# A fused DeltaNet and MLP-Mixer kernel: another order of its job pieces from the 705th on

## The chip, the cores and the metric

The kernel runs on one core of one Trainium2 chip. The metric is the device time of one execution in microseconds (us), as the median of several runs. PE is TensorE (PEld its weight loads), DVE VectorE, ACT ScalarE, POOL GpSimd, and SP the engine whose queue issues the DMAs.

## The reference, cut to what matters

Four batches of 768 positions go through a DeltaNet recurrence with 8 heads of 48 features. Its output, seen as 768 x 384 for each batch, goes through an MLP mixer with a token part and a channel part. Everything is fp32.

```python
k_n = k / (np.linalg.norm(k, axis=-1, keepdims=True) + 1e-06)
for t in range(S):                      # S = 768, state is 48 x 48 per head
    y[:, :, t] = q_t @ state
    state = state + beta_t * outer(k_t, v_t - state.T @ k_t)
...
h = np.maximum(x.T @ w_tok1, 0.0) @ w_tok2      # x: (768, 384) of one batch
u = x + h.T
out = u + np.maximum(u @ w_ch1, 0.0) @ w_ch2    # 384 -> 1536 -> 384
```

## The kernel before, in words

The recurrence is worked in chunks of 64 positions, two chunks to a unit u of 128, so there are 24 units and 48 chunk steps t, twelve to a batch. The kernel is written as jobs, each a Python generator that issues a few instructions and yields; one such stretch is a *piece*. There are 2543 pieces. One long string, `order` (line 1239), says by hand in which order the pieces are issued: `r12*5` means five pieces of job r12. Nothing is reordered after that. Each engine, and SP's DMA queue, works through its own instructions in the order of the string, and waits with semaphores where it needs another's result. So the string alone decides what stands ahead of what on each engine.

The jobs that matter here:

- `k{u}`, `v{u}` load keys, queries and values by SP's queue. The last piece of `v{u}` scales the values on POOL (line 426).
- `p{u}` prepares norms and scales; `c{u}` (and `d{u}` for the first twelve units) forms the Gram matrices on PE as small tiles (line 453, tile p_g), four pieces, and scales them on DVE (line 459).
- `t{u}` sends the triangular blocks to DRAM, `i{n}` inverts them for a round of up to four units on DVE (lines 681 and 686: a pair of dependent operations to a piece, 30 pairs), and `f{u}` fetches them back (line 653). `j{u}` joins the half blocks on PE in 32-row tiles (lines 785 to 834).
- `r{t}` is one chunk step of the recurrence, below.
- `m{b}` is the mixer of batch b: full 128-row tiles on PE, in lines 1060, 1073, 1083 (turns), 1140 for the first batch, 1032 for the others (a fast product with 15 sums in place of 18 products), and 1162. DVE adds the results (1044, 1077, 1091), ACT copies and clips.
- `w{j}` rounds one piece of the weights; `s` sums weight blocks; `x`, `z`, `Y` keep PE warm.

A step of the recurrence is a chain across engines, with a piece at almost every link:

```python
for p, i, r, _ in heads:                               # "k": 8 matmuls, four pieces
    nc.tensor.matmul(p_k[r, p], kqt[f, p, cc, 0], s0[f, p])                    # L862
nc.vector.tensor_tensor(out=rest, in0=p_k, in1=vsts[u][:, :, cc], ...)         # L869
for p, i, r, o in heads:                               # "y": 16 matmuls
    nc.tensor.matmul(p_y[o, p], kqt[f, p, cc, 1], s0[f, p], ...)               # L882
    nc.tensor.matmul(p_w[r, p], gm[r, 2 * p + cc, TC], rest[r, p])             # L886
nc.scalar.copy(w_t, p_w)                                                       # L892
for p, i, r, o in heads:                               # "s": 16 matmuls
    nc.tensor.matmul(p_s[PAR[i], p], gm[r, 2 * p + cc, 0:C], w_t[r, p])        # L900
    nc.tensor.matmul(p_y[o, p], gm[r, 2 * p + cc, GC], w_t[r, p], ...)         # L901
nc.vector.tensor_tensor(out=s1, in0=s0, in1=p_s, op=ALU.subtract)              # L909
nc.scalar.mul(y[...], p_y[...], ...)                                           # L914
```

The step t + 1 begins with the state s1 of step t. Each matmul of fp32 shows as two records in the profile, so k has 16 records and y and s have 32 each, of 48 or 64 rows and 64 columns. A whole step is ten pieces: four for k, then rest, y, w_t, s, s1 and the output. The first step of a batch (t = 0, 12, 24, 36) has no k and starts from the values. The text calls the bursts of step 31 k31, y31 and s31. Mixer b can start once the steps of its batch are written, and its pieces are put between the bursts of the later steps.

PE's work is thus of two kinds: full 128 x 128 tiles (mixer, transposes) and small tiles (Gram, joins, recurrence).

Of the kernel before, what the change touches and what calls it, by code (L numbers as in the profile page):

```python
# [23 lines left out]
def kernel(  # L24
# [1217 lines left out]
    c1*2 d1 k2 p2*2 c1 t0 d1 c1*2 d1*3 t0 p2*8 c2*2 w2 d2 c2*3 Y d2 w2 k3*6 p3 d2*2  # L1242
    p3 d2 t1*3 x p3*7 c3 k4*5 k7 w13 w18*2 d3*2 v1*2 v0*2 c3*3 v0 c3 d3*3 t0 p4*2
    t2*3 x t3*2 p4*2 x t3 i0*2 w13 p4*2 w18 w17*2 i0 k4 i0*9 p4 i0*2 p4*2 c4 k8
    c4*3 w13*2 w6*2 k5*2 v0 k6 k5*2 i0*2 d4*2 k5 x z d4*3 c4 z*2 p5*2 k5 t4 p5 h0
    h1 h0 w8*2 h1 Y i0 f0 Y p4 f1 h2*2 p5*3 f0*2 w6 h0*5 k6*5 p6 z f2*2 k8*3 p5 w6
    p5 p3 p5 j0*3 f1*2 h1*5 j0*2 w8*2 w17 f2 h2*3 v0 t4*2 w17 r0*5 p6 h2*2 c5*2 v1
    w11*2 j1 p5 k7*2 c5 k7 c5 r0 c5 r0*2 w14*2 v1 w11*2 k7*2 p7 d5*5 r1*5 w14*2
# [28 lines left out]
    r21*3 p15 r21*2 p16*4 j12 j13 k17*3 r21 j12 r21 p16 k17*3 m0*3 r21*3 m0 r22*2
    k17 r22 v11 k17 r22 k17*3 c16*4 r22*3 m0 c16*2 r22*3 t15 m0 r23*4 s p17*2 r23
    p16 p17*3 m0 p17 r23 k17 p17 t16 p17 m0*2 t16*2 t14*3 c17*2 t16 c17*3 r23 t14
    r23 c17 m0*2 s m0*3 t15*3 t17 s*4 t17*3 s*2 k18 m0*3 f12 i4*2 r23 i4*3 m0*2 i4  # L1280
    m0*2 v12*4 i4*2 k18 v12 k18*2 i4 k18 j13 m0*2 j13 r24*5 f13 j13*2 i4*4 r24 m0
    k18 m0*2 k18*2 v13*2 k18*2 r24 i4*2 k18*2 p18*2 i4 m0*3 r25 p18*2 r25*3 p18 i4
# [14 lines left out]
    m1*3 p23 m1*2 r35 m1 r35 p23*2 m1*6 t22*2 m1*2 c23*3 m1*2 c23*2 r35 c23 m1 v18
    f18*2 m1 t23*4 m1*2 r35 m1*6 j18*3 v18 j19 m1 v18 j19 f20 m1 j20 i6*4 f19 m1*3
    v18 j19 r36*4 j20 i6*2 r36*4 i6*5 m2 r37*3 f20 r37*2 i6*2 v20 f21 m2*2 f21 j21
    f21 r37*2 m2 i6*2 r37 m2*2 r37 r38*4 j20 i6*5 v19*5 r38 m2*2 r37 i6*4 r38 j21  # L1300
    r38*3 m2*3 r39*5 r38 m2*3 r39*2 m2*7 r39*2 m2*4 r40 j21 r40*4 i6 v21 i6*6 m2*2
    i6 r39 v21 m2*7 r40*2 j21*2 r40*3 m2 r41*5 m2*5 r41*2 m2*5 r41*3 m2*3 f22 m2
# [42 lines left out]
```

## Time and profile before

| | before |
|---|---|
| time, median of 3 runs | 639.9 us (639.62 to 640.89) |
| span of the profiled execution, first to last instruction | 636.9 us |
| PE busy | 608.5 us, 96% |
| DVE busy | 447.9 us, 70% |
| ACT busy | 268.0 us, 42% |
| POOL busy | 107.2 us, 17% |
| mean granted TensorE clock | 0.976 |

The times of the profile count from the span's start. The span is 3.0 us shorter than the median of the runs: the runs' time also holds what lies around the first and last instruction. A busy PE is an engine with some matmul in its pipeline; the time that it loses between matmuls of different kinds counts as busy too, so such losses have to be read from the starts of the matmuls and not from the busy share.

### The profile page before, as it was taken

The numbers are of one execution on the slowest core, as the hardware profiler recorded it, in microseconds if no ns is written. First come the engines' busy times: TensorE is split into PE (matmuls) and PEld (weight loads), VectorE is DVE, ScalarE is ACT, GpSimd is POOL, SyncE is SP. The second block draws the span as 40 slices with busy tenths as digits, with TensorE's granted clock in tenths as the row PEclk, the third lists the DMA queues.
The fourth block names the chain that finished last, engine by engine and source line by source line (L and its number), as shares of the span: only waits on it lengthen the run. The fifth ranks groups of instructions, "written<-read, shape, count | busy, mean of one in ns | idle before, by whom it ended". The sixth has DMA issues, their size and how long they took to land.

```text
span 636.9 us, 21542 instructions
## 1 busy us (share of the span) xinstructions
PE 608.5 (96%) x9132; PEld 531.5 (83%) x9132; DVE 447.9 (70%) x1132; ACT 268.0 (42%) x693; POOL 107.2 (17%) x146
## 2 busy tenths in 40 slices
PE   8488988899999999999999999999999999999997
PEld 5367877668898988859889999769999987999997
DVE  4987876967999658988969987776728253373643
ACT  7758785447523342215624323325334130232240
POOL 2348354235210211111111001000010000000000
PEclk9978796999999999999999999999999999999999
DMA  9686666666543355344454223202020000000000
GB/s 201 127 148 151 153 142 153 162 135 162 110 113 89 71 116 101 76 109 79 90 103 95 43 82 58 48 5 42 5 53 2 27 2 0 26 1 26 2 26 26
DMA packets 135776, 50.27 MB, mean 79 GB/s; under 512 B 114656, under 2 KB 130144, under 8 KB 135680
## 3 DMA queue, kind: packets, MB, share of 16 engines
q1 hardware_dynamic: 135680, 48.89, 35.2%
q8 instruction: 72, 1.18, 0.8%
q14 instruction: 24, 0.20, 0.1%
HBM read 39.42 MB, written 9.44 MB: 77 GB/s over the span
## 4 chain that ended last, share of the span: by engine, by line
PE 82%; DVE 7%; ACT 4%; DMA 3%; issue 2%; POOL 1%; SPq 1%; ACTq 0%; DVEq 0%; POOLq 0%
PE p_o L1162 26%; PE p_r L1032 20%; PE p_c L1140 8%; PE p_h L1073 5%; PE p L1060 4%; PE p_k L862 3%; PE p_g L453 3%; PE p_y L882 3%; PE p_s L900 3%; PE p_w L886 1%; DVE sub L681 1%; DVE x L686 1%; PE p_y L901 1%; PE p_ut L1083 1%; PE p_z L785 1%
## 5 line engine op out<-in xcount | busy, mean ns | idle before, releaser
L1162 PE MATMUL p_o<-wc,r 128*128 128x192 f32 x720 | 126.1, 329 | 0.6 <-ACT u_t L1087 0.6
L1162 PEld LDWEIGHTS p_o<-wc,r 128*128 128x128 f32 x720 | 116.8, 190 | 2.7 <-ACT u_t L1087 1.1
L1044 DVE TENSOR_TENSOR r<-r,p_r 128x512 f32<-128x512 f32 x90 | 59.8, 684 | 38.1 <-PE p_r L1032 34.3
L1091 DVE TENSOR_TENSOR xb<-xb,p_o 128x192 f32<-128x192 f32 x84 | 29.3, 350 | 57.8 <-PE p_o L1162 57.3
L1041 ACT COPY r<-p_r 128x512 f32<-128x512 f32 x54 | 31.3, 585 | 85.7 <-PE p_r L1032 76.1
L686 DVE TENSOR_TENSOR x<-x,sub 128x84 f32<-128x84 f32 (+24 forms) x178 | 59.4, 334 | 6.1
L681 DVE TENSOR_TENSOR sub<-x 128x84 f32<-128x84 f32 (+24 forms) x178 | 58.0, 326 | 6.8 <-DMA x<-n_dram 2.3
L1162 PE MATMUL p_o<-wc,s 128*128 128x192 f32 x288 | 51.5, 331 | 0.3 <-DVE xb L1091 0.3
L1140 PE MATMUL p_c<-u_t,wc 128*128 128x256 f32 x216 | 51.0, 386 | 0.2 <-ACT u_t L1087 0.2
L1162 PEld LDWEIGHTS p_o<-wc,s 128*128 128x128 f32 x288 | 46.7, 190 | 1.4 <-DVE xb L1091 0.6
L1048 ACT ACTIVATE r<-r 128x512 f32<-128x512 f32 x54 | 34.0, 631 | 26.7 <-DVE r L1044 26.2
L426 POOL TENSOR_TENSOR v_st<-v_st,nrm 128x384 f32<-128x384 f32 x24 | 20.1, 838 | 146.3 <-DMA v_st<-in_v_dram 109.3
L1140 PEld LDWEIGHTS p_c<-u_t,wc 128*128 128x128 f32 x216 | 39.7, 190 | 6.0 <-ACT u_t L1087 0.4
L516 POOL TENSOR_TENSOR mb<-mask_c,cs 128x512 f32<-128x512 f32 x20 | 21.2, 1062 | 138.9 <-DVE cs L494 138.6
L914 ACT ACTIVATE xb<-p_y 64x192 f32<-64x192 f32 x96 | 31.2, 325 | 23.6 <-PE p_y L901 12.2
L892 ACT COPY w_t<-p_w 128x192 f32<-128x192 f32 x48 | 15.2, 316 | 58.0 <-PE p_w L886 57.5
L1032 PE MATMUL p_r<-u_t,wc 128*128 128x128 f32 x288 | 38.7, 277 | 0.0
L453 PE MATMUL p_g<-kq 48*64 48x128 f32 (+1 forms) x704 | 33.6, 281 | 3.8 <-ACT kq L529 3.3
L1032 PE MATMUL p_r<-t_d,wc 128*128 128x128 f32 x288 | 37.3, 280 | 0.0
L1032 PEld LDWEIGHTS p_r<-u_t,wc 128*128 128x128 f32 x288 | 35.3, 192 | 0.4
L1060 PE MATMUL p<-xb,w 128*128 128x384 f32 x96 | 34.9, 511 | 0.0
L1032 PEld LDWEIGHTS p_r<-t_d,wc 128*128 128x128 f32 x288 | 34.0, 192 | 0.8
(184 smaller groups left out, 1212.2 us busy)
## 6 DMA issues: line engine op xcount, KB each, us to landing
d<-in_moe_w_ch_dram SPq DMA_DIRECT2D x24, 384.0 KB, 3.5
v_st<-in_v_dram SPq DMA_DIRECT2D x96, 48.0 KB, 2.7
out_dram<-xb SPq DMA_DIRECT2D x23, 192.0 KB, 1.9
kst<-in_k_dram SPq DMA_DIRECT2D x64, 48.0 KB, 2.9
n_dram<-gm SPq DMA_DIRECT2D x72, 32.0 KB, 2.4
pads<-in_k_dram SPq DMA_DIRECT2D x24, 96.0 KB, 2.9
pads<-in_q_dram SPq DMA_DIRECT2D x24, 96.0 KB, 2.9
gm<-w_dram SPq DMA_DIRECT2D x72, 32.0 KB, 2.1
```

Source lines behind the costliest of these rows:

```text
L453: nc.tensor.matmul(p_g[PAR[i ^ cc], p], kqt[f, p, cc, 0], kqt[f, p, cc])
L681: nc.vector.tensor_tensor(out=tmp, in0=y[:, :, 0:s, s : s + 1].to_broadcast([n, k, s, w]), in1=y[:, :, s : s + 1, s + 1 : m].to_broadcast( ...
L686: nc.vector.tensor_tensor(out=y[:, :, 0:s, s + 1 : m], in0=y[:, :, 0:s, s + 1 : m], in1=tmp, op=ALU.add,)
L914: nc.scalar.mul(y[:, :, D * i : D * i + D], p_y[PAR[1 - i]], 1.0 if c else -1.0)
L1032: nc.tensor.matmul(p[:, i], pieces[i // width][:, at : at + 128], f[f"u{n}"], start=first and i == 0, stop=True, skip_group_check=True,)
L1041: nc.scalar.copy(o, p)
L1044: nc.vector.tensor_tensor(out=o, in0=o, in1=p, op=ALU.add if sign > 0 else ALU.subtract)
L1048: nc.scalar.activation(o, o, ACTF.Relu)
L1060: nc.tensor.matmul(p_1[dh], piece_of(w1, c, 0)[:, dh * 128 : (dh + 1) * 128], xb[:, c], start=(c == 0), stop=(c == NCH - 1),)
L1073: nc.tensor.matmul(p_h, piece_of(w2, j, c * 128)[:, c * 128 : (c + 1) * 128], r1[j], start=(j == 0), stop=(j == NDH - 1),)
L1140: nc.tensor.matmul(p_c[:, k], piece_of(wc1, cb, f * 128)[:, f * 128 : (f + 1) * 128], u_t[:, cb], start=(cb == 0), stop=(cb == NCB - 1),)
L1162: nc.tensor.matmul(p, a[:, m], wc2[:, m, j], start=(start and i == 0), stop=(i == NM - 1), skip_group_check=True,)
```

## The change

Only the string `order` changes. The first 704 pieces and the last 159 (all of mixer 3) stand as before; between them the same pieces come in another order. Each job's own pieces keep their order, and every engine gets the same instructions as before, with the same shapes. In the new string more pieces with small tiles, of the Gram, join and recurrence jobs, stand next to each other, where the old one has a mixer piece between them. The first part and the end of the change, as they stand in the two strings (lines of the diff that only break differently are left out):

```diff
-    ... k11*2 v5 r10*3 i2 w4 i2*3 w15*3 w19*2 i2 w19 m0
-    i2 w12 r10*2 m0*2 r11 r10 p11 k12*4 w19 p11 p10 k12*2 p12 Y i2 w25 r11*3 d10*4
-    r11*2 v7 c10*3 w15 k12 i2*2 w21 i2*4 v6*3 r11*2 i2*3 k11 r11 v7*4 i2*4 c10
+    ... k11*2 v5 w15 p10 m0 k12 w12 w15 i2*3 r10*3
+    i2*4 k12 w4 k11 m0 r10 w12 w25*2 w12 i2 m0 r10 r11 k12*3 r11 c10 r11*2 r10
+    i2*2 w12 r11 i2*10 c10*3 w21 f7 k12 f6 d10 c10 r11*2 d10 p11 f6*2 d10*2 r11*2
...
-    r12 m0 w23*4 j8 r12 t10 r12 t10*2 r13 p10 w23 r13*4 w20*2 p11*3 p12*2 w20*2
+    j6*2 m0 j7*3 w25 v6 w25*4 v6 f9 m0 v6 w20 p10 w27 r12*5 p12 r12*3 p11 c11 w27
+    c11*4 w20*2 w21*2 r13*4 m0 r13*3 w20 f8*2 j8 t10*3 j8*2 k12 w15 f8 f9 k12
...
-    r30*3 t18*4 f17*2 f16 t19*2 c20*3 t20*3 r31*5 p21*3 m1*2 r31 p21
-    r31*3 c21*2 p21 c21 m1 t19 j17 t20 c21*3 m1 t21*4 r32*4 m1*12 j17 m1 v16*4 r32
+    p20*2 m1*4 r30 m1 c20 r30*2 r31*2 k21*6 p21*2 r31*3 c20*5 t20*2 r31 t20*2 m1
+    v16*2 m1 v16*3 m1 r31*3 p21*4 r31 m1*14 k22*2 r32*5 m1*3 k22 m1*2 p21 r32*2
+    m1*3 r32*2 k22 c21*2 r33*4 r32 r33 c21*4 t18 r33*2 m1 t18 k22*4 p21 k22*4
+    p22*3 r33*3 j17*2 p22*2 r34*4 v17*5 r34 m1*2 p22*2 r34*2 c22*2 r34*3 c22*3 Y
...
-    m2*2 f23*3 j23 r43*2 m2*6 f23 m2*11 v22 m2*4 r43*2 j23 r44*2 r43 r44 j23 r44
-    m2*5 v22*4 r44*3 m2*3 r44*3 m2*5 r45*5 m2*9 r45*2 j23 r45*3 m2*2 j23 m2*9 p23
-    v23*3 m2 r46*4 m2*2 v23*2 r46 m2*9 r46*2 m2*2 r46*3 m2*7 r47*5 m2*6 r47 m2 r47
-    m2*2 r47 m2*6 r47 m3*6 m2*5 m3*6 m2*11 m3*3 m2 m3*159
+    r42 r41 r42*4 m2 r42 m2 r42*3 m3 r42 r43*4 f22*3 j22*2 r43*3 m3 f23*3 r43 f22
+    j23 j22 j23*2 r43*2 r44 f23 r44*3 v22*5 m3 r44*6 j23*2 r45*9 r46*2 r45 v23*5
+    r46*8 m2 r47*5 m3 r47*4 m3*170
```

The mixer pieces that stood between the bursts of steps 44 to 47 now stand earlier or later in the string.

More of the change, by code (lines that the diff above doesn't have):

```diff
@@ L1241 @@
     w10 p0*2 z w3 w2 c0*3 p0 w3*2 d0*2 w3 c0 p1 c0 d0*3 k2*3 v1 p1*2 w18 k2*2 p1*2
[L1242 to L1248, printed above, removed]
+    c1*2 d1 k2 p2*2 c1 t0 d1 c1*2 d1*3 t0 p2*8 c2*2 w2 d2 c2*3 Y d2 w2 k3*6 p3
+    d2*2 p3 d2 t1*3 x p3*7 c3 k4*5 k7 w13 w18*2 d3*2 v1*2 v0*2 c3*3 v0 c3 d3*3 t0
+    p4*2 t2*3 x t3*2 p4*2 x t3 i0*2 w13 p4*2 w18 w17*2 i0 k4 i0*9 p4 i0*2 p4*2 c4
+    k8 c4*3 w13*2 w6*2 k5*2 v0 k6 k5*2 i0*2 d4*2 k5 x z d4*3 c4 z*2 p5*2 k5 t4 p5
+    h0 h1 h0 w8*2 h1 Y i0 f0 Y p4 f1 h2*2 p5*3 f0*2 w6 h0*5 k6*5 p6 z f2*2 k8*3 p5
+    w6 p5 p3 p5 j0*3 f1*2 h1*5 j0*2 w8*2 w17 f2 h2*3 v0 t4*2 w17 r0*5 p6 h2*2 c5*2
+    v1 w11*2 j1 p5 k7*2 c5 k7 c5 r0 c5 r0*2 w14*2 v1 w11*2 k7*2 p7 d5*5 r1*5 w14*2
     p6*2 t5 j1 t5*2 r1*2 j1 j2 p7 h3*2 r1*3 p6*3 i1*2 r2*5 k8*2 f3*2 w9 k9*3 j1*2
@@ L1257 @@
     w29 w27*2 r8*2 w29*3 j4*2 r8 w22*4 t9*4 r8*3 p10 h5*2 k11 h5 j5 Y i2 r9*3 r8
-    r9*2 i2*4 j5 i2*3 r9*2 i2 h5 k12*2 j5 Y r9*2 m0 v6 k11 j5 p9 w4*2 r10*3 i2*2 j5
-    k10 r10 p10*4 w4 v5 i2 v5*3 r9 k11*2 v5 r10*3 i2 w4 i2*3 w15*3 w19*2 i2 w19 m0
-    i2 w12 r10*2 m0*2 r11 r10 p11 k12*4 w19 p11 p10 k12*2 p12 Y i2 w25 r11*3 d10*4
-    r11*2 v7 c10*3 w15 k12 i2*2 w21 i2*4 v6*3 r11*2 i2*3 k11 r11 v7*4 i2*4 c10
-    k12*3 m0*4 c10 m0*2 w25 m0 w12 d10 f6*4 f7*2 p11*2 m0*3 w12 w21 w12 p12 p11*2
-    m0*2 f7 w21*2 j6*2 j7 v6 p12 w25*3 f8*2 w27*2 m0 j6 j7*2 m0 r12*5 f8 f7 j8*2
@@ L1277 @@
[L1277 to L1282, printed above, removed]
@@ L1297 @@
[L1297 to L1302, printed above, removed]
@@ L1303 @@
-    f22*2 v21*3 r42*4 j22*2 r42 m2*3 r42*2 m2*2 f22 m2*5 r42*3 m2*2 j22 m2*4 r43*5
-    m2*2 f23*3 j23 r43*2 m2*6 f23 m2*11 v22 m2*4 r43*2 j23 r44*2 r43 r44 j23 r44
-    m2*5 v22*4 r44*3 m2*3 r44*3 m2*5 r45*5 m2*9 r45*2 j23 r45*3 m2*2 j23 m2*9 p23
-    v23*3 m2 r46*4 m2*2 v23*2 r46 m2*9 r46*2 m2*2 r46*3 m2*7 r47*5 m2*6 r47 m2 r47
-    m2*2 r47 m2*6 r47 m3*6 m2*5 m3*6 m2*11 m3*3 m2 m3*159
+    r9*2 i2*4 j5 i2*3 r9*2 i2 h5 k12*2 j5 Y r9*2 m0 v6 k11 j5 p9 w4*2 r10*3 i2*2
+    j5 k10 r10 p10*4 w4 v5 i2 v5*3 r9 k11*2 v5 w15 p10 m0 k12 w12 w15 i2*3 r10*3
@@ new lines @@
+    i2*4 k12 w4 k11 m0 r10 w12 w25*2 w12 i2 m0 r10 r11 k12*3 r11 c10 r11*2 r10
+    i2*2 w12 r11 i2*10 c10*3 w21 f7 k12 f6 d10 c10 r11*2 d10 p11 f6*2 d10*2 r11*2
+    m0 f7 m0*2 p11 m0 f8 f7 d10 f7 m0*3 p11*4 j6 f6 w21 p11 p12*2 v6 p11 m0*3 p11
+    j6*2 m0 j7*3 w25 v6 w25*4 v6 f9 m0 v6 w20 p10 w27 r12*5 p12 r12*3 p11 c11 w27
+    c11*4 w20*2 w21*2 r13*4 m0 r13*3 w20 f8*2 j8 t10*3 j8*2 k12 w15 f8 f9 k12
+    r13*3 p12*2 w15 m0 d11 r14*4 v7*2 d11*3 v7*2 w19*2 v7 r14*3 w19*2 m0 d11 r14
+    f9 k12 p12 k12 p12 f9 c12*3 w32*2 j9 w32*2 w31*2 k13*4 r14 r15*3 r14 w31 w30*2
@@ new lines @@
+    p12 w30*2 r15*2 c12*3 m0*3 w31*2 m0 r15*2 k13*8 p13*3 j9*2 p13*3 r15 v8*4
+    w23*4 p13*2 w23*2 r15*2 w31 t11*3 w31 m0*8 r16*4 m0*2 w29 v10*3 v8 r16*2 w33*6
+    r16 c13*6 r16*2 m0*4 w27 s*2 r17*4 r16 w33 t11 t10 w29 k14*8 m0*4 r17*3 t12*3
+    t13*4 t12 i3*3 j9*2 i3 w23 i3*3 p14*2 r17*2 m0*2 p14*3 m0*3 i3*2 s i3*7 k15*4
+    i3*3 m0*5 i3*5 m0*4 k15*4 p15*2 v10 m0*6 v9*3 i3 v9*2 r18*2 p15 k14*4 p14*2
+    k15*4 p14 r18*3 r17 i3 m0*5 i3*6 f13 f10*3 f13 m0 r18 f11*3 m0*3 r18*4 p15 f10
+    c14*6 s r19*4 p15 j10 p15 m0*6 r19*2 j10 r19*2 j11 j10 j11*2 v10 r19 t14 r20
@@ new lines @@
+    t14*2 r20*4 r19 m0*2 r20*2 f12*3 j12 f11 j12 f12 k16*8 p15 k16*2 s j12 s*3
+    r20*3 m0 r21*5 v11*5 p15 c15 p16 c15 k16 r21 c15*3 r21*4 k16 c15 t15*2 p16*4
+    m0*2 p16 m0*4 f13 p16 r22*4 j13*2 v12*4 r22*2 k17*2 m0*2 t15 k17*7 p17*3 t15
+    r22 m0*5 k17*2 m0 j13 r22*3 k17 c16*5 r23*5 c16 t16*4 p17*2 k18*3 m0*4 r23*2
+    s*3 v14 m0*2 p17 r23 p17*2 p16 v12 r24 r23 r24*2 c17 r24 c17*5 t14 r24 t17
+    r24*2 t17*3 i4 m0*2 s*5 m0 i4*7 m1*9 i4*3 m1*6 k18*5 p18 r25*5 m1*11 p18 m1*2
+    r24 m1*6 i4*3 p18 k18 m1*2 k18 m1*2 p18*2 k18 k19*2 m1*2 k19*4 p18 m1 r25*2
@@ new lines @@
+    k19 m1*9 v14 m1 v14 m1*9 r25*3 m1*6 f13 j13 i4*3 v13 j13 v13*4 r26*5 k18 m1 i4
+    m1 i4*2 m1*5 p18 m1 k19 m1 i4 m1 i4*2 m1*2 i4*6 m1*10 p18 r26*2 i4*3 f17*4 f14
+    c18*6 t18*2 f15*4 f16 r26*2 m1*2 f14*2 r26 f14 m1*23 r27*5 m1 j14 m1*5 r27*2
+    j14*2 j15 r27*2 p19*5 m1 r27 v14 j15*2 v14 r28*4 k19*4 m1*3 f16*2 r28 f16
+    r28*2 v15*4 j16*3 j17 v15 r28*2 k20*2 p19*3 k20 m1 r28 k20*3 r29 k20*4 r29*4
+    m1*3 r29 k20*2 p20*5 c19*6 r29*2 m1*8 r29*2 r30*4 m1 j17*2 r30*3 p20 k21*6
+    p20*2 m1*4 r30 m1 c20 r30*2 r31*2 k21*6 p21*2 r31*3 c20*5 t20*2 r31 t20*2 m1
@@ new lines @@
+    v16*2 m1 v16*3 m1 r31*3 p21*4 r31 m1*14 k22*2 r32*5 m1*3 k22 m1*2 p21 r32*2
+    m1*3 r32*2 k22 c21*2 r33*4 r32 r33 c21*4 t18 r33*2 m1 t18 k22*4 p21 k22*4
+    p22*3 r33*3 j17*2 p22*2 r34*4 v17*5 r34 m1*2 p22*2 r34*2 c22*2 r34*3 c22*3 Y
+    c22 t21 v18 r35*5 t21 t19*4 t21*2 k23*2 i5*2 m1 p22 r35*2 m1*2 r35*2 m2*4 i5
+    m2*2 m1 i5 k23 i5*10 k23*9 i5 m2 p23*2 m1 m2 p23*5 m2*26 i5*2 m2*4 i5 m2*20
+    c23*4 m2*8 i5*3 m2*2 c23 m2*3 i5*5 m2*3 i5*3 m2*8 i5*3 t22*4 f18*4 m2*16 v18
+    m2 j18 f19*3 m2*3 f20*2 m2*7 v18 c23 t23 f20 p23 v18 j18 m2*2 j19 j18 m2*8 j19
@@ new lines @@
+    m2*5 j19 m2 v18 r36*4 f19 j20*2 r36*2 t23*3 j20 i6*2 v19*3 i6*5 m2 r36 m2 r37
+    r36 i6*4 r37*4 m2*5 r37 m2 r37 i6 v19*2 m2 r37 i6*2 m2*6 r37*2 m2 f21*3 i6*3
+    r38*5 i6 m2*7 j21 m2*2 r38 m2 r38 m2*4 r38 m2 f20 j21 r38*2 r39*4 i6 f21 m2
+    r39*2 i6 m2*5 r39*4 v20*3 i6*3 v20 m2 v20 r40*3 j21 r40*2 m2*2 r40 m2 i6 r40
+    v21*2 r40 v21*2 r40*2 m2 i6*4 m2*2 r41*5 i6 j21*2 i6*2 r41 m2 i6 r41*3 m2 v21
+    r42 r41 r42*4 m2 r42 m2 r42*3 m3 r42 r43*4 f22*3 j22*2 r43*3 m3 f23*3 r43 f22
+    j23 j22 j23*2 r43*2 r44 f23 r44*3 v22*5 m3 r44*6 j23*2 r45*9 r46*2 r45 v23*5
```

25 lines of the change are left out of this document (removed).

## The prediction

> **What bounds the kernel now.** I read the page first, then the busy time by stage, then PE's waits after 115 us. There the first burst stands whose place differs: the kernel's 705th job piece.
>
> ```profile
> PE 608.5 (96%) x9132; PEld 531.5 (83%) x9132; DVE 447.9 (70%) x1132; ACT 268.0 (42%) x693; POOL 107.2 (17%) x146
> PEclk9978796999999999999999999999999999999999
> PE 82%; DVE 7%; ACT 4%; DMA 3%; issue 2%; POOL 1%; SPq 1%; ACTq 0%; DVEq 0%; POOLq 0%
> 300.00:400.00 100.00, 98.52 (x1578) 93.64 (x1577) 84.50 (x208) 39.14 (x99) 11.80 (x18) 1.00 0.36 78
> PE p_k L862 <- DVE s_t L909: 1.3, 2, 0.9
> PE p_y L882 <- ACT xb L914: 1.3, 2, 0.9
> PE p_g L453 <- DVE kq L369: 0.6, 1, 0.6
> PE p_s L900 <- ACT w_t L892: 0.5, 1, 0.5
> PE p_w L886 <- DVE rest L869: 0.4, 1, 0.4
> ```
>
> PE carries 82% of the chain, runs at full clock after the start and is almost never idle: in 300 to 400 us it is busy for 98.5 of 100, with DVE at 84.5. After 115 us its listed waits come to about 5 us. So the order can only help if it makes PE's own queue cheaper, and it hurts wherever PE stands and waits. Both can be priced.
>
> **What a burst costs beside its own matmuls.** Here a lone y burst (32 records of p_y and p_w, one piece of a recurrence step) stands between full-tile products.
>
> ```profile
> 304.96 1.16 PE L1032 MATMUL p_r<-u_t,wc 128*128 128x128 f32 x8
> 306.05 0.25 PE L882 MATMUL p_y<-s_t,kq 48*64 48x48 f32 x1
> 306.20 0.22 PE L882 MATMUL p_y<-s_t,kq 48*64 48x48 f32 x1
> 306.49 0.22 PE L882 MATMUL p_y<-s_t,kq 48*64 48x48 f32 x1
> 306.66 1.16 PE L1032 MATMUL p_r<-t_d,wc 128*128 128x128 f32 x8
> ```
>
> Each row has start, length, line and count. Five groups of four records lie between 306.20 and 306.49, so four take 0.058 and the burst's 32 take 0.47. Eight p_r follow each other at 0.112 and the last is 0.275 long, which makes 1.06, but the rows say 1.16: after a burst one more 0.10 is lost. The last p_r ahead begins at 304.96 + 1.16 - 0.275 = 305.85; the burst should follow at 305.96 and begins at 306.05, 0.09 late. From its begin to the next p_r are 0.61. So it costs 0.09 + 0.61 + 0.10 = 0.80, of which 0.47 is work and about **0.34 is the price of going in and out**. Two bursts of equal tile size side by side pay it once. A join of 64-row with 32-row bursts (lines 785 to 834) saves less:
>
> ```profile
> 403.28 0.67 PE L886 MATMUL p_w<-v_st,gm 64*64 64x48 f32 x16
> 403.87 0.21 PE L785 MATMUL p_z<-t,gm 32*32 32x32 f32 x1
> ```
>
> The last p_w begins at 403.28 + 0.67 - 0.22 = 403.73 and p_z 0.14 later: 0.14 is paid at each such joint. The Trainium skill ("TensorEngine Tiling (Array Packing)", Key Properties) says that a change of tiling mode drains TensorE. If each joint of 64 and 32 rows therefore cost as much as going out to full tiles, the saving below would be 0.34 x (16 - 6) = 3.4 instead of 4.6; the two rows above speak for the smaller price.
>
> In PE's list before, from that piece on, the small bursts form 88 stretches between full-tile products, with 30 joints of 64 and 32 rows inside; in the new list they form 72, with 36. The matmuls are the same ones. 16 x 0.34 - 6 x 0.14 = **4.6 us saved**. Nothing has to hide this: it is PE's own time.
>
> **What the joins cost.** Within a step the bursts are a chain: k (p_k), then DVE's rest, y, then ACT's w_t, s (p_s with p_y), then DVE's s_t, and the next step's k. Full-tile pieces between them cover that trip through another engine. The trace has one trip with no cover, in step 31:
>
> ```profile
> 319.98 0.22 PE L886 MATMUL p_w<-rest,gm 64*64 64x48 f32 x1
> 320.28 0.32 ACT L892 COPY w_t<-p_w 128x192 f32<-128x192 f32 x1 [0.18 <-PE p_w L886]
> 320.65 0.25 PE L900 MATMUL p_s<-w_t,gm 64*64 64x48 f32 x1 [0.46 <-ACT w_t L892]
> L869 DVE TENSOR_TENSOR rest<-p_k,v_st 128x192 f32<-128x192 f32 x35 | 12.3, 352 | 9.8 <-PE p_k L862 7.7 <-DMA gm<-w_dram 0.8 <-POOL v_st L426 0.7
> L909 DVE TENSOR_TENSOR s_t<-s_t,p_s 128x192 f32<-128x192 f32 x31 | 10.8, 348 | 12.0 <-PE p_y L901 12.0
> ```
>
> From the last p_w to the first p_s are 0.67, where the next record of a stretch would follow within about 0.07 (an estimate between 0.015, a record's turn above, and 0.14, the joint). A bare trip costs 0.60 through ACT, and through DVE, whose 0.35 stands for ACT's 0.32, 0.63. That is more than the 0.34 that the join saves. While PE waits, everything behind it in its queue stands too, the mixer's products first, and no other engine has work that PE could use sooner.
>
> The Trainium skill ("Perfetto Trace Analysis", Optimizing Tensor Performance) asks for independent matmul groups in rotation, so that ACT and DVE empty one while the next runs. It speaks against joining bursts of one chain; the 0.67 above agrees.
>
> *The end of the recurrences.* The new order reads r44*6 j23*2 r45*9 r46*2 r45 v23*5 r46*8 m2 r47*5 m3 r47*4. In PE's queue this is y44, s44, j23, k45, y45, s45, k46, y46, s46 without one full-tile product, then one product, k47, one product, y47, s47. Seven trips are bare (y44-s44, three from k45 to k46, two from k46 to s46, y47-s47): 7 x 0.61 = 4.3. The trip past j23 is covered. Before, m2 and j23 pieces lay in all of them. **+4.3**, between 3.5 (a trip at 0.5) and 5.3.
>
> *Step 12.* r12*5 p12 r12*3 puts s12 directly behind y12: **+0.6**.
>
> *Steps 10 and 11.* Here DVE is late, not PE.
>
> ```profile
> 115.14 0.34 DVE L869 TENSOR_TENSOR rest<-p_k,v_st 128x192 f32<-128x192 f32 x1
> 115.41 0.38 DVE L681 TENSOR_TENSOR sub<-x 128x228 f32<-128x228 f32 x1
> 118.02 0.41 DVE L681 TENSOR_TENSOR sub<-x 128x240 f32<-128x240 f32 x1
> 115.54 0.25 PE L886 MATMUL p_w<-rest,gm 64*64 64x48 f32 x1 [0.42 <-DVE rest L869]
> 116.15 1.56 PE L1060 MATMUL p<-xb,w 128*128 128x384 f32 x4
> 122.02 0.26 PE L862 MATMUL p_k<-s_t,kq 48*64 48x48 f32 x2 [0.93 <-DVE s_t L909]
> ```
>
> The new order puts i2*3 ahead of step 10's rest. Three steps of the inversion take 118.02 - 115.41 = 2.6, so y10 can start 2.6 later. One m0 piece (the row with 1.56, of which some 1.3 to its next start) is moved ahead of y10, so 1.3 is PE idle. Three m0 pieces in all stand ahead of k11 in both orders, so k11 inherits that 1.3: eight inversion steps now precede its s_t where six did, 1.7 by the same rows, less a weight piece of 0.35 that no longer does. In step 11 two more steps (1.7) stand ahead of the rest, with k11 and c10 as cover (some 0.9 and DVE's trip): 0.6 more. **+1.9**, between 0.5 (cover found elsewhere) and 3.5.
>
> *Partly covered trips.* Eight trips (12 to 13, 14, twice in 21, 32 to 33, 33, 34, 34 to 35) have half a Gram job as cover.
>
> ```profile
> 301.82 1.07 PE L453 MATMUL p_g<-kq 48*64 48x128 f32 x32
> 302.71 0.20 PE L901 MATMUL p_y<-w_t,gm 64*64 64x48 f32 x1
> 287.04 0.60 PE L862 MATMUL p_k<-s_t,kq 48*64 48x48 f32 x13
> 288.98 0.82 PE L1032 MATMUL p_r<-u_t,wc 128*128 128x128 f32 x5
> ```
>
> 32 Gram records take 302.71 - 301.82 = 0.89, so 16 cover 0.45 of 0.6: 8 x 0.15 = 1.2. For mixers 2 and 3, which begin with nothing beside their transposes and sums, and for DVE queues ahead of c17, r36 and m0's products I put 1.2 more, an estimate of four waits at half a bare trip. What goes is the cluster at steps 30 and 31 (p_k's second wait 0.4, p_g 0.6, p_s 0.5): -1.5. Net **+0.9**, between -1.5 and 2.5.
>
> *The sum*: -4.6 + 4.3 + 0.6 + 1.9 + 0.9 = +3.1. The profiled execution's span is 636.9, which becomes 640.0; the median of the runs, 639.9, lies 3.0 above the span, for what lies around it. **643.0 us.**
>
> **The rivals.**
>
> (a) *The early waits vanish: faster.* PE's waits for step 10 and k11 are 0.9 + 0.4 + 0.9 by the waits above. m0's piece moved ahead of y10 may cover them all, if DVE does its three inversion steps before that piece ends, within 1.3 us instead of 2.6 (from there it decides). The early term is then -2.2 instead of +1.9, the partial trips come to 0.3: -4.6 + 4.9 - 2.2 + 0.3 = -1.6, 638.3 us. Against it: dependent DVE rows 0.43 apart, with no gap to use. 0.11.
>
> (b) *Savings and waits cancel.* The early and partial terms are zero: -4.6 + 4.9 = +0.3, 640.2 us. 0.09.
>
> (c) *A load comes late at the end.* v22 and v23 are now loaded behind a store of m2 and eight returns from the inversion, on SP's one queue.
>
> ```profile
> gm<-w_dram SPq DMA_DIRECT2D x72, 32.0 KB, 2.1
> v_st<-in_v_dram SPq DMA_DIRECT2D x96, 48.0 KB, 2.7
> L426 POOL TENSOR_TENSOR v_st<-v_st,nrm 128x384 f32<-128x384 f32 x24 | 20.1, 838 | 146.3 <-DMA v_st<-in_v_dram 109.3
> ```
>
> Step 44's rest needs v22 landed (2.7 after its issue) and scaled (0.84). I count about 1 us to spare. If SP is 2 to 3 late, PE adds that: 645.5 us. 0.14.
>
> (d) *Bursts overlap.* The Trainium skill (the same Tiling page, Key Properties) lets different tiles work in parallel. As a mechanism here: k uses two of four tiles and would hide beside Gram matmuls, ten k bursts at 0.45. That would give 643.0 - 4.5 = 638.5 us. The rows above speak against it: k with Gram and y takes 288.98 - 287.04 = 1.94, just 0.89 + 0.47 + 0.14 and 0.44 for k. 0.03.
>
> **How the numbers follow.** The forecast has 0.63, from 641.3 to 645. Bounds of the unknown terms together reach 640 and 647, which takes in (b) and (c); (a) and (d), 0.14, lie below. A measurement tells 0.2%, 1.3 us, from no change. Faster by more: (a), (d), less what of them stays within: 0.12. Within: (b) and edges: 0.10. Slower: 0.78.
>
> **What would show it.** Right: PE waits for w_t, rest and s_t at some 0.5 each in an unbroken row of bursts at steps 44 to 47; longer waits at steps 10 and 11; fewer, longer stretches elsewhere, with joined bursts 0.34 cheaper. Wrong: no idle PE at steps 44 to 47, a joint that saves more than 0.34, or waits of over a microsecond for a DMA.

## The result, and the profile after

The changed kernel takes **672.6 us** (median of 4 runs, 668.6 to 675.5) beside 640.0 for before (639.6 to 640.9): 1.0504 times as long, 95% interval 1.0463 to 1.0544. The forecast was 643.0, with a range from 640 to 647. It had the direction, and 3 of the 32.5 us. Medians, ranges and ratios here and below leave out single runs that lie more than 1.5% above the fastest of their kernel (one run each of three kernels).

The profiled execution has a span of 670.8 us (before 636.9) and a mean granted clock of 0.957 (before 0.976). These are the lines of the changed kernel's page, and the stage from 300 to 400 us of its busy time by stage, that answer to those of before:

```profile
PE 624.3 (93%) x9132; PEld 541.4 (81%) x9132; DVE 455.4 (68%) x1132; ACT 270.4 (40%) x693; POOL 109.5 (16%) x146
PEclk9889896899999999899998999999999995999999
PE 60%; DVE 17%; DMA 7%; ACT 6%; SPq 5%; issue 3%; POOL 1%; DVEq 0%; ACTq 0%; POOLq 0%
300.00:400.00 100.00, 97.24 (x1501) 92.33 (x1499) 76.26 (x180) 42.01 (x105) 12.94 (x17) 0.97 0.29 64
```

PE keeps its work, but only 60% of the chain that ends last is PE's now, where it was 82%. DVE, DMAs and SP's queue have come in, so where PE waits, what it waits for is often late itself. PE's waits after 115 us in the changed kernel (us in total, times, longest):

```profile
PE p_o L1162 <- DVE xb L1091: 5.2, 6, 2.0
PE p_w L886 <- DVE rest L869: 5.0, 5, 1.9
PE p_s L900 <- ACT w_t L892: 2.6, 5, 0.6
PE p_s L900 <- issue: 2.0, 1, 2.0
PE p_k L862 <- DVE s_t L911: 1.2, 1, 1.2
PE p_k L862 <- DVE s_t L909: 1.0, 2, 0.6
```

With the smaller ones they come to 22, where before had 5. The second thing that is new is in the row PEclk: single slices of 8 and one of 5. The stages in which the granted clock falls (the third number from the end is the clock):

```profile
118.00:122.00 4.00, 4.00 (x62) 2.26 (x65) 3.72 (x11) 2.21 (x5) 0.32 (x1) 0.59 0.47 118
265.00:272.00 7.00, 7.00 (x93) 6.91 (x93) 3.74 (x9) 0.65 (x2) 1.92 (x3) 0.53 0.11 18
364.00:371.00 7.00, 5.76 (x37) 5.14 (x37) 2.06 (x4) 2.11 (x7) 0.24 (x1) 0.53 0.21 44
555.00:569.00 14.00, 11.74 (x184) 8.80 (x188) 2.04 (x6) 2.35 (x8) 0.00 (x0) 0.52 0.04 15
```

By the clock's own records it is at half for 30.7 us in all there (the windows above take in a little of full clock too, so they show 0.52 to 0.59); before has no such stretch between 111.5 us and its last two microseconds.

**Where the time went, by place.** From the starts of PE's 9132 records I counted how much later each comes than the usual spacing of its two kinds (0.112 for a p_r after a p_r, 0.163 for p_o, 0.148 from a small tile to a full one, and so on). Unlike idle time, this holds slow matmuls too.

| late starts, us | 115 to 200 | 200 to 300 | 300 to 400 | 400 to 547 | 547 to end | sum |
|---|---|---|---|---|---|---|
| before | 4.5 | 0.9 | 2.3 | 0.9 | 2.7 | 11.2 |
| changed | 11.3 | 9.5 | 6.6 | 5.2 | 12.1 | 44.7 |

The 33.5 us more are close to the 33.9 by which the span grew, and they are spread over the whole kernel. Four places show the kinds of cause. The first is SP, DVE and PE around 260 us, in the order of time:

```profile
255.67 3.30 SPq L413 DMA_DIRECT2D kst<-in_k_dram  x4
260.88 0.52 ACT L481 ACTIVATE ksq<-kst 128x384 f32<-128x384 f32 x1 [2.27 <-DMA kst<-in_k_dram]
261.43 0.55 DVE L484 TENSOR_REDUCE ksum<-ksq 128x8 f32<-128x384 f32 x1 [7.31 <-ACT ksq L481]
263.83 1.24 PE L1162 MATMUL p_o<-wc,s 128*128 128x192 f32 x6 [1.96 <-DVE xb L1091]
```

SP's queue is at work for nearly all of 245 to 261 us, and the keys of unit 17 are issued late on it. ACT squares them on landing, and DVE stands at its next instruction in order, a reduction of these squares, for 7.31 us. The mixer's add (xb) that PE needs is queued behind it on DVE, so PE stands for 1.96 although neither keys nor squares are anything it wants now. The second place is step 44, the one that rival (c) named:

```profile
545.00 6.86 SPq L413 DMA_DIRECT2D v_st<-in_v_dram  x8
550.67 0.83 POOL L426 TENSOR_TENSOR v_st<-v_st,nrm 128x384 f32<-128x384 f32 x1 [24.91 <-DMA v_st<-in_v_dram]
551.53 0.36 DVE L869 TENSOR_TENSOR rest<-p_k,v_st 128x192 f32<-128x192 f32 x1 [3.18 <-POOL v_st L426]
551.68 0.31 PE L882 MATMUL p_y<-s_t,kq 48*64 48x48 f32 x2 [0.96 <-ACT xb L914]
```

Eight loads in one row take SP 6.86 us. DVE's rest waits 3.18 for POOL; PE has other work for 2.2 of it and stands for 0.96. (The p_y row names ACT; its partner p_w starts at 551.94, as soon as the rest is done.) The third is the row of bare trips behind it, with only each burst's first record shown:

```profile
553.04 0.25 PE L900 MATMUL p_s<-w_t,gm 64*64 64x48 f32 x1 [0.43 <-ACT w_t L892]
555.32 0.25 PE L886 MATMUL p_w<-rest,gm 64*64 64x48 f32 x1 [0.35 <-DVE rest L869]
556.70 0.34 PE L900 MATMUL p_s<-w_t,gm 64*64 64x48 f32 x1 [0.48 <-ACT w_t L892]
558.26 0.77 PE L862 MATMUL p_k<-s_t,kq 48*64 48x48 f32 x10 [0.46 <-DVE s_t L909]
559.87 0.34 PE L886 MATMUL p_w<-rest,gm 64*64 64x48 f32 x1 [0.52 <-DVE rest L869]
561.45 0.34 PE L900 MATMUL p_s<-w_t,gm 64*64 64x48 f32 x1 [0.48 <-ACT w_t L892]
```

From 555.6 on a lone small matmul takes 0.34 instead of 0.25: the clock is at half. The fourth place is a wait for no engine, in the chain of the changed kernel, inside an unbroken y28 j16 s28:

```profile
363.28 1.96 issue
```

### The profile page after: what moved, and what is told of

It is laid out like the page before. It is cut to its first block, busy times and chain, and to the rows that moved or that the text cites. A ratio compares the mean times of both kernels' runs of the same rounds, so it can differ in the third digit from the quotient of the medians.

```text
span 670.8 us, 21570 instructions
## 1 busy us (share of the span) xinstructions
PE 624.3 (93%) x9132; PEld 541.4 (81%) x9132; DVE 455.4 (68%) x1132; ACT 270.4 (40%) x693; POOL 109.5 (16%) x146
## 3 DMA queue, kind: packets, MB, share of 16 engines
q8 instruction: 72, 1.18, 0.8%
## 4 chain that ended last, share of the span: by engine, by line
PE 60%; DVE 17%; DMA 7%; ACT 6%; SPq 5%; issue 3%; POOL 1%; DVEq 0%; ACTq 0%; POOLq 0%
PE p_r L1032 18%; PE p_o L1162 17%; PE p_h L1073 5%; PE p L1060 4%; DVE x L686 3%; DVE sub L681 3%; DMA d<-in_moe_w_ch_dram 3%; PE p_k L862 3%; PE p_s L900 2%; PE p_g L453 2%; DVE s L1114 2%; SPq L628 2%; PE p_y L882 2%; PE p_c L1140 2%; DMA x<-n_dram 2%
## 5 line engine op out<-in xcount | busy, mean ns | idle before, releaser
L1162 PE MATMUL p_o<-wc,r 128*128 128x192 f32 x720 | 132.5, 336 | 1.5 <-DVE xb L1091 0.8
L1162 PEld LDWEIGHTS p_o<-wc,r 128*128 128x128 f32 x720 | 119.4, 194 | 4.9 <-DVE xb L1091 1.1
L1041 ACT COPY r<-p_r 128x512 f32<-128x512 f32 x54 | 31.6, 585 | 92.9 <-PE p_r L1032 79.6
L1162 PE MATMUL p_o<-wc,s 128*128 128x192 f32 x288 | 54.6, 341 | 4.4 <-DVE xb L1091 4.4
L1162 PEld LDWEIGHTS p_o<-wc,s 128*128 128x128 f32 x288 | 48.5, 196 | 6.8 <-DVE xb L1091 5.9
L453 PE MATMUL p_g<-kq 48*64 48x128 f32 (+1 forms) x704 | 37.5, 291 | 3.5 <-ACT kq L529 2.8
L1060 PE MATMUL p<-xb,w 128*128 128x384 f32 x96 | 37.9, 541 | 0.8 <-DVE xb L1091 0.8
L900 PE MATMUL p_s<-w_t,gm 64*64 64x48 f32 x640 | 29.5, 233 | 7.5 <-ACT w_t L892 5.2
```

The source lines that it names most:

```text
L453: nc.tensor.matmul(p_g[PAR[i ^ cc], p], kqt[f, p, cc, 0], kqt[f, p, cc])
L1041: nc.scalar.copy(o, p)
L1060: nc.tensor.matmul(p_1[dh], piece_of(w1, c, 0)[:, dh * 128 : (dh + 1) * 128], xb[:, c], start=(c == 0), stop=(c == NCH - 1),)
L1162: nc.tensor.matmul(p, a[:, m], wc2[:, m, j], start=(start and i == 0), stop=(i == NM - 1), skip_group_check=True,)
```

## The experiments

**Only the end made bare.** Before's order, with the mixer pieces of steps 44 to 47 moved behind them and v23 loaded ahead; then the same with two dummy matmuls in each of the seven bare trips.

```diff
-    v22*4 r44*3 m2*3 r44*3 m2*5 r45*5 m2*9 r45*2 j23 r45*3 m2*2 j23 m2*9 p23 v23*3 ...
+    v22*4 p23 v23*5 r44*6 j23 r45*9 r46 r45 j23 r46*9 m2 r47*5 m2 r47*4 ...
```

> The order of before, with only the end of the recurrences made as in the change: the bursts from y44 to s46 stand side by side without a mixer piece, y47 and s47 too; v23 is loaded earlier so that no load is late. Theory W (a bare trip costs its wait and nothing else): seven trips at 0.61 less seven ins and outs at 0.34 is +1.9, 642 us, granted clock 1.0 throughout. Theory C (the sparse stretch also halves PE's granted clock for the windows after it, as the trace after shows 0.52 in 555 to 569 us): +1.9 and half of some 10 to 14 us more, 646 to 649 us, with a granted clock near 0.5 in that stretch.

> The same order, with two dummy full-tile matmuls (128 columns of zeros, their result is not used) in each of the seven bare trips, so that PE has something to do while the chain waits. Theory W: as e1 or up to 1 us slower, 642 to 643. Theory C, if the clock follows PE's activity: the granted clock stays at 1.0 and the time is 642 to 644, 3 us or more below e1. If the clock halves all the same, zeros or too little work do not count as activity and the time stays with e1.

Bare: 648.2 us (645.3 to 651.8), 1.0119 times before (1.0059 to 1.0180). With dummies: 645.7 (644.3 to 647.7), 1.0072 (1.0042 to 1.0102). The busy time by stage of the first, and the row PEclk of the second:

```profile
482.00:491.00 9.00, 6.99 (x128) 6.09 (x126) 2.02 (x5) 3.26 (x10) 0.00 (x0) 0.50 0.02 4
```

```profile
PEclk9979796999999999999999999999999999999999
```

The bare end alone costs 7.5 us, and its clock is 0.50; with dummies the clock stays up and it costs 5.0. The two intervals overlap, but the profiled executions say the same: from one and the same matmul, some 165 us ahead of the end, to the last instruction they take 7.3 and 5.1 us more than before's. So about 2.5 went with the lower clock. The other 5 are not the forecast's 4.3 by themselves: they hold the trips, less the 2.4 that seven joins should save, and the dummies' own time, 3.1 at most (14 at 0.22, as the control below gives it).

**The changed order with its end covered again**: eleven m2 pieces out of the row m2*26 moved to steps 42 to 47, seven of them into the bare trips and four to where m3 pieces stood, which go behind. The cut shows the part from step 45 on.

```diff
-    ... r45*9 r46*2 r45 v23*5 r46*8 m2 r47*5 m3 r47*4
+    ... r45*5 m2 r45*2 m2 r45*2 m2 r46*2 r45 v23*5 r46*3 m2 r46*2 m2 r46*3 m2 r47*5 m2 r47*2 m2 r47*2
```

> The changed order with eleven of mixer 2's pieces moved from one earlier block of twenty-six into the trips of steps 42 to 47, and mixer 3's first pieces after them. Theory W: 2 us below the changed kernel, 670. Theory C: the waits of 547 to 575 us (some 8.9 us lost there) and the 13.7 us at half clock go: 658 to 663 us.

700.8 us (698.2 to 703.2), 1.0937 times before (1.0877 to 1.0997): a miss. In its waits PE loses 14.7 us to the mixer's adds, 8.3 in one piece:

```profile
PE p_o L1162 <- DVE xb L1091: 14.7, 7, 8.3
```

```profile
472.12 0.25 DVE L681 TENSOR_TENSOR sub<-x 128x84 f32<-128x84 f32 x1
472.41 0.24 DVE L686 TENSOR_TENSOR x<-x,sub 128x84 f32<-128x84 f32 x1
472.57 0.35 DVE L1091 TENSOR_TENSOR xb<-xb,p_o 128x192 f32<-128x192 f32 x1
```

These three rows are DVE's at the end of the long wait: the inversion steps, with some of the mixer's sums between them, follow each other without a gap from 462 us on, and the add that PE needs stands behind them. Taking eleven pieces out of the row puts each piece of mixer 2 that follows, up to step 47, further back in the order, and its adds behind other steps. The edit measured that, and says nothing of the end.

**The changed order up to step 24, before's from step 25 on.**

> The changed order up to the first burst of step 25 (some 280 us), then the rest as before has it. If the losses are local to where they show (11.3 us lost in 115 to 200 us against 4.5 before, 9.5 against 0.9 in 200 to 300, and 10 us at half clock), this takes 650 to 655 us. If the loss comes from the end alone (rival), 638 to 642 us.

681.1 us (678.1 to 682.9), 1.0625 (1.0566 to 1.0685): a miss too. At the seam the busy time by stage and the waits of 300 to 340 us read:

```profile
300.00:340.00 40.00, 19.31 (x358) 16.59 (x357) 29.75 (x79) 8.28 (x25) 5.05 (x7) 0.66 0.32 68
```

```profile
PE p_w L886 <- DVE rest L869: 9.8, 2, 5.0
PE p_y L882 <- ACT xb L914: 5.3, 1, 5.3
```

Loads and inversion steps fall into a lump where the two orders meet, and PE is idle for half of 40 us. Ahead of the seam this run repeats the early losses; behind 340 us it has little more than before. So the loss isn't in one place, and these two orders can't be cut and joined without a loss at the cut.

**Single places of the changed order undone.** The dummies in the seven trips; one m1 piece moved into y28 j16 s28; p17 three pieces later; v7's loads ahead of step 13.

```diff
-    v15*4 j16*3 j17 ...                  (m1 piece)
+    v15*4 m1 j16*3 j17 ...
-    k17*7 p17*3 r22 m0*4 ...             (p17)
+    k17*7 r22 m0*5 k17*2 m0 p17*3 j13 ...
-    r13*4 m0 r13*3 ... v7*2 d11*3 ...    (v7)
+    v7*4 r13*4 m0 r13*3 ... d11*3 ...
```

> The changed order with two dummy full-tile matmuls (128 columns of zeros, result unused) in each bare trip of steps 44 to 47. The trips stay bare, only the clock should stay up. Theory C (sparse work halves the clock, the 13.7 us at half clock behind 555 us do some 8 us of work that full clock does in 4): 4 us less than the changed kernel, 668 us, and no half-clock window at the end of the recurrences. Theory W: 672 or slower.

> The changed order with one m1 piece (half a product) moved from behind y28 j16 s28 into that unbroken run of 256 instructions. Theory I (PE works through small tiles faster than its instructions arrive; the 2.0 us that it stood for issue at 363.3 us is a 16 KB block of instructions that was not there yet): the wait goes, and with it the 6.8 us at half clock behind it: 4 to 5 us less than the changed kernel, 667 to 668 us. Rival (the wait has another cause): it stays, 672 us.

> The changed order with three pieces of p17 (ACT's squares, DVE's row sums, ACT's roots) moved behind the six m0 pieces that follow them, so that the loads of k17, late on SP's queue, have landed when DVE reaches them. Theory D (DVE stood 7.3 us for that load with m0's additions queued behind it, PE stood 2.1 us for those and 6.8 us at half clock followed): 4 to 5.5 us less than the changed kernel, 667 to 668 us. Rival (DVE is short of time there and the wait comes back at c17 and step 24): 671 to 673 us.

> The changed order with the four loads of v7 moved some thirty pieces ahead, before step 13. Theory D (step 14's wait of 1.4 us, and those of 0.6, 0.8 and 0.8 behind it, come from values that SP issued too late): 1.5 to 3.5 us less than the changed kernel, 669 to 671 us. Rival (SP's queue has no gap between 138 and 158 us, so what is moved ahead makes f8, f9 and the weights late by as much): 672 us with the wait at another step.

| | median, us | range | ratio to before (95%) |
|---|---|---|---|
| dummies at the end | 669.8 | 668.6 to 676.9 | 1.0507 (1.0440 to 1.0573) |
| m1 piece | 668.5 | 667.9 to 671.0 | 1.0463 (1.0436 to 1.0490) |
| p17 later | 673.0 | 671.7 to 681.3 | 1.0553 (1.0487 to 1.0619) |
| v7 earlier | 671.0 | 668.3 to 674.0 | 1.0493 (1.0447 to 1.0539) |

No median stands clear of the spread: the m1 piece has the lowest, 4 us down as its theory said, and its interval still meets the changed kernel's (1.0463 to 1.0544). What its profile shows is clear: the issue entry of 1.96 is gone, and the longest left in the chain there is

```profile
363.11 0.04 issue
```

All six other runs that keep this burst unbroken (the end covered, the other three of these, and the light inversion and light loads below) show PE standing there again, for 1.8 to 2.4 us.

With p17 later the wait at 263.8 us is gone, and this one has come five microseconds behind it, as the rival said:

```profile
PE p_g L453 <- ACT gm L807: 2.5, 1, 2.5
```

**All four undone together, and dummies at every long wait.** The second moves nothing: sixty dummies stand where PE waits longest (ahead of y10, y14, two pieces of mixer 0, s28, and in the seven trips).

> The changed order with four of its edits undone together: one first-mixer piece (m1) moved into the unbroken y28 j16 s28, p17 three pieces later, v7's loads ahead of step 13, and two dummy 128 x 128 matmuls put into each of the seven bare trips at the end. Theory S (the losses are separate and add): from the single runs -4 for the m1 piece, -1.5 for v7, 0 for p17, and -3 to -5 for the end by the profile of the run with dummies: 661 to 665 us. Rival B (the order is a coupled queue, so that a wait taken away at one place comes back at the next): 667 to 672 us, no better than the best single edit.

> The changed order with nothing moved; only dummy 128 x 128 matmuls are added where PE stands longest: ten pieces ahead of y10, eight ahead of y14, eight and ten ahead of the mixer pieces 65 and 93 of the first batch, ten ahead of s28, and two in each of the seven bare trips at the end. Every wait on DVE, ACT and the loads stays. Theory C (the clock that drops to half after a wait is a loss of its own beside the wait): no record of half clock after 115 us, and some 10 to 14 us less, 658 to 663 us, so that about 20 of the 32 us remain as waits. Rival W (the half clock falls into time in which PE has to wait anyway, so it costs little): the waits grow by what the clock saves, 668 to 674 us.

671.6 us (667.3 to 676.4), 1.0519 times before (1.0450 to 1.0588), and 670.3 (665.2 to 672.9), 1.0469 (1.0420 to 1.0518): by the medians, no gain of note from either. Runs of these orders spread by 3 to 10 us, some of it from the first 110 us, which no edit touches (the first product of mixer 0 starts at 108.0 to 112.6 us in their profiled runs). So I counted the profiled executions from that product on, to the same piece of each. The table has the time that each gains (-) or loses on the changed kernel up to there:

| up to | dummies at the end | m1 piece | p17 | v7 | four together | dummies everywhere |
|---|---|---|---|---|---|---|
| mixer 0, piece 95 | -0.1 | 0.7 | 4.7 | -1.0 | 1.6 | 3.9 |
| mixer 1, piece 101 | -1.1 | -0.1 | 3.9 | -1.9 | 0.8 | 3.0 |
| mixer 1, piece 137 | -0.8 | -3.2 | 2.9 | -2.8 | -2.9 | 0.2 |
| mixer 2, piece 147 | -0.3 | -2.6 | 1.8 | -2.2 | -2.1 | 0.3 |
| mixer 3, piece 41 | -3.4 | -1.3 | 0.5 | -1.4 | -6.5 | -2.7 |
| end | -3.4 | -1.3 | 0.5 | -1.4 | -6.5 | -2.7 |

The first column belongs to an order that is the changed kernel's up to the bare trips, so what it shows above its last two rows is how far one execution differs from another: 1 us here, and up to 4 at places ahead of the first row. Single entries of that size say nothing. Two gains come back wherever their edit is in: about 3 between pieces 101 and 137 of mixer 1 (PE's stand in the unbroken burst and the half clock behind it), and 3 to 4 over the end. The clock itself was held up nearly everywhere by the sixty dummies:

```profile
PEclk9879795999999979999999999999999999999999
552.00:570.00 18.00, 16.55 (x433) 13.02 (x426) 3.20 (x9) 6.65 (x24) 1.81 (x3) 1.00 0.14 30
```

and yet nothing was gained up to piece 95. So of the 10 to 14 us that the expectation put to the clock, only some 6, with the waits beside them, can be shown. Early on either the rival holds, and full clock just meets the next late DVE result sooner, or the dummies took what the clock gave: the 36 ahead of piece 95 are 8 us of PE's time (at 0.22) wherever they last longer than the wait. No run tells these two apart.

**The price of going in and out, by itself.** Before's order with 34 dummies, each dividing a k or a Gram burst; and the control with the same dummies between mixer products.

```diff
-    r31*4 ...            (in 34 bursts)
+    r31*2 x r31*2 ...
```

> The order of before with 34 dummy 128 x 128 matmuls, each put into the middle of a k burst or of a Gram burst between steps 13 and 42. Each takes 0.22 us by itself (two records of 0.112) and divides one stretch of small tiles into two. The prediction's price of going in and out of small tiles, 0.34, gives 34 x (0.22 + 0.34) = 19.0: 659 us, and 11.6 more than the control with the same dummies beside mixer products. Rival P (the price is only that of a joint, 0.14): 34 x 0.36 = 12.2, 652 us, and 4.8 more than the control.

> The control: the order of before with the same 34 dummy 128 x 128 matmuls, each put between two mixer products of full tiles near the places of the other kernel. By both theories 34 x 0.22 = 7.6: 647 to 648 us.

657.3 us (654.9 to 659.4) and 646.4 (644.8 to 647.4): 1.0292 (1.0256 to 1.0327) and 1.0119 (1.0092 to 1.0147) times before. The difference is 11.0, which is 0.32 a division; the forecast's price was 0.34. A divided burst of the first kernel, then a dummy of the control:

```profile
304.43 0.43 PE L862 MATMUL p_k<-s_t,kq 48*64 48x48 f32 x8
304.79 0.49 PE L225 MATMUL p_warm<-warm 128*128 128x128 f32 x2
305.21 0.43 PE L862 MATMUL p_k<-s_t,kq 48*64 48x48 f32 x8
```

```profile
294.47 0.39 PE L225 MATMUL p_warm<-warm 128*128 128x128 f32 x2
294.70 1.06 PE L1032 MATMUL p_r<-t_d,lent 128*128 128x128 f32 x8
```

Between full tiles the dummy holds PE for 0.23; inside the burst the next k comes 0.42 after it, and the dummy itself came late.

**DVE's queue or SP's.** Each pair makes one kind of work cheap in both orders. The inversion keeps its operations and their places, on one row of the block, so the inverse is not computed:

```diff
-    in0=y[:, :, 0:s, s : s + 1], ...   # and out, in0 of the add
+    in0=y[:, :, 0:1, s : s + 1], ...
```

The loads of kst and v_st take rows of 768 bytes instead of 192, so other values arrive.

> The changed order, with the late rounds of the triangular inversion made light: each pair of DVE operations works on one row of the block instead of all rows so far, so the inverse is not computed. The 30 pairs of each of five rounds, some 0.65 us a pair before, keep their places and waits and take perhaps a third of it. Theory D (PE waits because DVE's inversion steps stand ahead of what PE needs): 12 us or more go, 655 to 660 us, and the waits on rest and xb fall by half. Rival L (the late loads on SP's queue set the waits): 4 us or less, 668 to 673 us.

> The order of before with the same light inversion. Both theories: it has 5 us of waits on PE after 115 us, so at most 3 us go, 636 to 640 us.

> The changed order, with the loads of values and of stacked keys from unit 8 on taken from rows of 768 bytes that lie together, instead of rows of 192 bytes; the bytes and the number of DMAs are the same, but the values that arrive are others. Rival L: SP's slots for these loads get shorter (v_st and kst took 0.5 to 1 us each), the waits behind them go (k17's 7.3 us on DVE, v7 and v22 on POOL), and 5 us or more are saved, 662 to 668 us. Theory D: within 3 us of the changed kernel, 669 to 675 us.

> The order of before with the same loads. Both theories: within 1.5 us of before, 638 to 641 us.

| | changed order | order of before |
|---|---|---|
| light inversion | 663.5 (661.0 to 668.7), 1.0388 (1.0318 to 1.0458) | 637.6 (633.9 to 642.3), 0.9966 (0.9930 to 1.0002) |
| light loads | 668.9 (664.7 to 671.0), 1.0453 (1.0392 to 1.0515) | 639.2 (637.3 to 640.7), 0.9990 (0.9965 to 1.0015) |

The groups of DVE's inversion, in the changed kernel and then in the changed order with light inversion:

```profile
L686 DVE TENSOR_TENSOR x<-x,sub 128x84 f32<-128x84 f32 (+24 forms) x178 | 58.9, 331 | 6.1
L681 DVE TENSOR_TENSOR sub<-x 128x84 f32<-128x84 f32 (+24 forms) x178 | 57.2, 321 | 14.6 <-DMA x<-n_dram 10.1
```

```profile
L682 DVE TENSOR_TENSOR sub<-x 128x28 f32<-128x28 f32 (+23 forms) x178 | 35.8, 201 | 16.3 <-DMA x<-n_dram 11.8
L687 DVE TENSOR_TENSOR x<-x,sub 128x28 f32<-128x28 f32 (+23 forms) x178 | 35.0, 197 | 6.1
```

45.3 us of work taken from DVE give 9.0 us in the changed order and 2.1 in that of before; of the 10.2 us that PE waits on the mixer's adds and the rests, 7.6 are left. So DVE's inversion steps are a part of the loss, between what theory D and rival L expected.

The loads give 3.6 and 0.4, but the changed kernel's interval meets this run's, and the edit hardly made them light. In the changed order SP's issues of kst and v_st from 115 us on take 74.6 us where they took 79.6, the longest wait for keys on DVE is still there (7.02 for 7.31), and 9.4 of the 10.2 us of PE's waits are left. So the pair does not test what the late loads cost; that stays open.

```profile
263.56 0.55 DVE L495 TENSOR_REDUCE ksum<-ksq 128x8 f32<-128x384 f32 x1 [7.02 <-ACT ksq L492]
```

**All of it together.**

> The changed order with all at once: the four edits (one m1 piece inside y28 j16 s28, p17 later, v7 earlier, dummy matmuls in the seven bare trips), the light inversion, which does not compute the inverse, and the light loads, which bring other values. Theory A (separate losses add): 672.6 less 9.0, 3.6 and 4 to 6 gives 653 to 657 us. Rival B (a coupled queue: one lateness hides the next): 661 to 666 us, little better than the light inversion alone.

> The order of before with the light inversion and the light loads together. Both theories: 636 to 639 us.

656.7 us (655.2 to 658.6), 1.0268 (1.0240 to 1.0296), beside 638.5 (635.8 to 641.6), 0.9977 (0.9951 to 1.0003), for before's order with both light changes. This is about what the sum of the parts gives (653 to 657), and not 661 to 666: the losses are mostly separate and add up. Of the waits on the mixer's adds and the rests, 10.2 us in the changed kernel, these are left (this kernel's lines lie 12 further down):

```profile
PE p_o L1174 <- DVE xb L1103: 0.5, 2, 0.3
PE p_w L898 <- DVE rest L881: 0.2, 1, 0.2
```

What remains is 18 us over the other order, at most 3.1 of it the dummies' own time. Its late starts come to 26.3 us, beside 10.4 for before's order with the light changes: 9.1 of them from 115 to 200 us, where of the four edits only v7's loads lie, and 5.3 from 200 to 300. At least half of the sum lies in starts that are late by less than 0.4 us. Which order of pieces sets these was not taken apart further and stays open.

## Why the prediction was right or wrong

**The price of the joins** (0.34) held: 0.32 by itself. No run isolates the 4.6 that 72 stretches in place of 88 should save. An estimate from PE's starts in the two traces, with each kind of step at its usual spacing, gives 4 to 5.

**The seven bare trips** (4.3): the late starts of these bursts are 0.56, 0.48, 0.69, 0.67, 0.73, 0.70 and 0.63, in all 4.5. **Step 12** (0.6): 0.76. **Step 10** (1.3 of PE's time): y10 starts 2.0 late (its wait before was 0.4), with three of DVE's inversion steps ahead of its rest, as written:

```profile
115.02 0.40 DVE L681 TENSOR_TENSOR sub<-x 128x228 f32<-128x228 f32 x1
117.52 0.35 DVE L869 TENSOR_TENSOR rest<-p_k,v_st 128x192 f32<-128x192 f32 x1
117.93 0.25 PE L886 MATMUL p_w<-rest,gm 64*64 64x48 f32 x1 [1.87 <-DVE rest L869]
```

**The step that failed is the fourth term, "partly covered trips" and what I called the net of the rest, put at +0.9.** Take the three named places (7.3 us) from the 44.7 of late starts and before's 11.2 from what is left: it should have been 26. (By the sum of the prediction, from the 32.5 us measured, it comes to 30; where the other 4 lie was not settled.) I worked it out trip by trip on PE's list, with DVE, ACT, POOL and SP taken to be ready whenever PE's own order was. I had looked at DVE's queue at steps 10 and 11 only, and at SP's only at the end. In both places it was late. The same reading, at every rest, xb and s_t, would have shown the inversion steps ahead of them (by the light inversion 7 us of the difference, 9.0 less 2.1, with an uncertainty of 5 to 6 us from the intervals) and loads of k, v and x that DVE and POOL meet in order, whose price no run isolates. Everything made light and the four edits together take 14 of the 32.5 us off the difference; the other 18 stay open. DVE's waits for such loads in the changed kernel after 115 us, where before has 1.1 and 1.3 us:

```profile
DVE sub L681 <- DMA x<-n_dram: 10.1, 4, 4.2
DVE ksum L484 <- ACT ksq L481: 8.9, 4, 7.3
```

The forecast did write down that waits of over a microsecond for a DMA would prove it wrong. These are such waits, one instruction away from PE. The range was too narrow by its own terms as well: the bounds given for the three uncertain ones add up to 638.4 and 647.2, not 640 and 647.

**"PE runs at full clock after the start"** was read from before and carried over to the changed kernel without a price for its loss. It cost 2.5 us at the bare end alone, and 3 to 4 in the changed kernel's. The four half-clock stretches are 3.4, 6.8, 6.8 and 13.7 us long, multiples of one length, and each comes behind a wait of some 2 us or a run of bare bursts. The Trainium skill ("TensorE: Matmul & The Clock Gate", Part 1: The HAM clock gate) gives a free-running window of about 3.4 us and half rate after an idle one. The lengths agree; the waits here, 1.87 to 1.96, are shorter than the window, so a whole idle window wasn't needed. Nor does every such wait bring the clock down: with the m1 piece moved, PE stood 2.44 us at 266 us and the clock stayed full.

**Rivals.** (c) was right in its mechanism, but small: y44 waited 0.96, not 2 to 3. (a) failed at once: y10 waited 1.87. Nothing was seen of (b) and (d). No rival held the case that came about, in which DVE and SP are late all along, and the range could not reach it.

## What to carry to other kernels

Where several in-order queues are scheduled by hand, price a new order on every queue: for each instruction that moves, ask what stands ahead of it on DVE and on the DMA queue, and when the data of *that* will have landed. A saving on the bound engine, here 0.32 us for a joined pair of bursts, is small beside the slack of the other queues that it uses up, and a stretch priced as "partly covered" needs a bound from those queues, not from the engine's own list. When an order fails in many places at once, make one kind of work cheap in both orders: the difference of the two gains tells more than undoing single places, whose waits can move on. Then look in the trace whether it did become cheap, as the loads here did not.
